# Transnormer attention and MLP mixer on one core: whole-tile attention for the first pair, reordered copies, earlier last stores

## The chip, the cores and the metric

The kernel runs on one core of a Trainium2 chip. The metric is the device time of one execution in microseconds (us). A core has a matrix engine (TensorE, PE in the profile, with its weight loads shown apart as PEld), a vector engine (DVE), a scalar engine (ACT), a general engine (POOL), and queues that issue DMAs (SP's, and ACT's own). Each engine runs its instructions in the order in which they were written; semaphores make one wait for another.

## The reference

For 8 batches of 576 tokens, with 8 heads of 64 columns:

```
kv  = einsum('bhsd,bhse->bhde', k, v)            # 64x64 per head
out = einsum('bhsd,bhde->bhse', q, kv)
x   = out / sqrt(mean(out*out, -1) + 1e-6) * g_norm   -> (8, 576, 512)

h   = relu(x^T @ w_tok1) @ w_tok2                # 576 -> 256 -> 576 tokens
u   = x + h^T
out = u + relu(u @ w_ch1) @ w_ch2                # 512 -> 1536 -> 512 channels
```

All activations are float32, and the MLP's weights come as float64 words, which the kernel decodes to float32 itself.

## The kernel before

**Pairs and tiles.** Batches are worked on in four pairs. Each batch has four tiles of 128 tokens and a rest of 64; the rests of a pair share a ninth tile. The work of a pair is: `kv` (k^T v per head, for one half of a batch's heads), `evict` (L348, from PSUM to `kvp`), `attend` (L357, q times kv), `gain` (L386, the product with g_norm, on DVE), `square` (L394, on ACT), `total` (L407, row sums on DVE), `mean`, `sqrt`, `invert` (L415 to L431), and then the scaling of x by the inverse root, on ACT as eight instructions of 64 columns (`scale`, L433) or on POOL as one (`scale_pool`, L440). Then `token_mixing` (L462): `tok1` into the four banks of the PSUM pool "h", a ReLU on ACT, and `tok2`, which either starts from zero (DVE then adds x) or is seeded: x is copied into PSUM first (`seed`, L483, on ACT), and the result is copied back by ACT.

**Quarters.** `attend` works by quarters of the array: 64 rows times 64 columns. `kvp` holds the 64x64 blocks of two heads above each other, and a step covers two tiles: one of its two banks (PSUM pool "o") gets the even heads of both tiles, the other the odd heads.

**The order.** The order on every engine is written out by hand, as lists of short names that `play` (L1018) runs from left to right: `start` (first pair's attention), `middle` (first pair's mixing with the second pair's attention), two `steady` lists and `last`. In the names, `kv00` is batch 0 of the pair, first half of the heads; `e00` its eviction; `l00` a load of k and v; `a0` to `a3` the attention of two tiles each, `a4` that of the rests; `g`, `q`, `t` gain, square and total; `m`, `r`, `i` mean, root and inverse of a group; `s` and `p` the scaling on ACT and on POOL; `h00` to `h11`, `hr` are `tok1`, `z2` is a seed and `u2` a `tok2`; `j14` is 14 small matmuls that only keep PE busy; `f` fetches a block of channel weights. A digit alone takes so many steps of the `rounding` stream, which decodes the channel weights block by block: an ACT scaling (L163) and six DVE instructions (L166 to L191); the scaling of the next block is issued with the fifth of them, the fetch of a later one with the last. The decoding of `w_tok2` is `w3x` and `w4x` in `middle`.

**After the mixing.** Channel mixing follows group by group as two nested fast matrix products of seven products each. `outer` (L722) builds one level; `put(place, ...)` sets a step beside a numbered product, `PLACE` orders the seven. With `onto=True`, for the very last of them (L883), its results are added straight to the output tile `xg` ("take", "write" and "put_on" are these additions). `store` (L985) and `store_rest` (L994) write the output: for the last group each issues one DMA on SP's queue and one on ACT's. Their places for the last group are in L967 to L970:

```
for place, steps in ((40, [xadd(1, 0, 4)]), (43, [xadd(0, 1, 6)]), (44, [radd(7, 6)]),
                     (46, [xadd(1, 0, 7)]), (47, [xadd(1, 1, 7)]), (49, [xadd(0, 1, 5)]),
                     (50, [xadd(1, 1, 5), do(store, g, xg, 1)]),
                     (52, [do(store_rest, xg, 1)]), (56, [do(store_rest, xg, 0)])):
```

Of the kernel before, what the change touches and what calls it, by code (L numbers as in the profile page):

```python
# [19 lines left out]
def kernel(  # L20
# [81 lines left out]
    v_in = [inp.tile([P, JJ, DH], F32, name=f"v_in{i}") for i in range(4)]  # L102
    kvp = [inp.tile([P, HP, D], F32, name=f"kvp{i}") for i in range(2)]
    u_dram = [dram.tile([J * P, DM], F32, name=f"u_dram{g}") for g in range(NG)]
# [226 lines left out]
    def attention(pair, groups):  # L331


        bank, stat, kv_ps = {}, {}, {}

        def kv(side, half):
            n = 4 * pair + 2 * side + half
            kk, vv = k_in[n % 4], v_in[n % 4]

            o = kv_ps[side, half] = ps["kv"].tile([P, 2, D], F32, name="ps_kv")  # L340
            for i in range(2):
                for j in range(JJ):
                    for h in range(2):
                        at = ds(i * P + h * D, D)
                        matmul(o[ds(h * D, D), i], lhsT=kk[:, j, at], rhs=vv[:, j, at],
                               start=(j == 0), stop=(j == JJ - 1), skip_group_check=True)

        def evict(side, half):  # L348
            o = kvp[side][:, 2 * half:2 * half + 2]
            if pair == 0:  # L350
                keep(nc.vector.tensor_copy(o, kv_ps[side, half]))
            else:
                copy(o, kv_ps[side, half])

        def attend(c):  # L357
            o = [ps["o"].tile([P, 2, HP, D], F32, name="ps_o", tag="o") for _ in range(2)]
            side = c // 2
            for t in range(2):  # L360
                for hp in range(HP):
                    for n in range(2):
                        for h in range(2):
                            r = ds(h * D, D)
                            matmul(o[h][ds(n * HF, HF), t, hp],
                                   lhsT=qT[2 * pair + side][r, hp, ds((2 * (c % 2) + t) * P + n * HF, HF)],
                                   rhs=kvp[side][r, hp], start=True, stop=True)
            for h in range(2):
                bank[c, h] = o[h].rearrange("p t k d -> p (t k) d")

        def attend_rem():
            o = [ps["o"].tile([P, HP, D], F32, name="ps_r", tag="o") for _ in range(2)]
            for hp in range(HP):
                for side in range(2):
                    for h in range(2):
                        r = ds(h * D, D)
                        matmul(o[h][ds(side * HF, HF), hp], lhsT=qT[2 * pair + side][r, hp, LO:],
                               rhs=kvp[side][r, hp], start=True, stop=True)
            for h in range(2):
                bank[4, h] = o[h]  # L380


        number = lambda c: HP if c == 4 else 2 * HP
        sq = {}

        def gain(c, h):  # L386
            if (pair, c) not in X:
                n = 1 if c == 4 else 2
                X[pair, c] = xps[pair % 2].tile([P, n, DM], F32, name="x", tag=f"x{n}",
                                                bufs=4 if n == 2 else 1)  # L390
            x = X[pair, c].rearrange("p t (k h d) -> p (t k) h d", h=2, d=D)[:, :, h]
            keep(nc.vector.tensor_mul(x, bank[c, h], g_sb.to_broadcast([P, number(c), D])))  # L392
# [8 lines left out]
        def stats_of(c):  # L401

            g = group(c)
            at = sum(2 * number(i) for i in g if i < c)
            return [t[:, ds(at, 2 * number(c))].rearrange("p (h k) o -> p h k o", h=2) for t in stat[g]]

        def total(c, h):  # L407
            g = group(c)
            if g not in stat:
                stat[g] = [stats.tile([P, sum(2 * number(i) for i in g), 1], F32, name=name)  # L410
                           for name in ("ms", "root", "inv")]
            keep(nc.vector.tensor_reduce(stats_of(c)[0][:, h], sq[c, h], axis=AX.X, op=ALU.add))  # L412
# [11 lines left out]
        def invert(g):  # L424
# [6 lines left out]
            keep(nc.vector.reciprocal(inv, root))  # L431

        def scale(c, t):  # L433
            x = X[pair, c][:, t].rearrange("p (k h d) -> p k h d", h=2, d=D)
            inv = stats_of(c)[2][:, :, ts(t, HP)]
            for k in range(HP):
                for h in range(2):
                    keep(nc.scalar.activation(x[:, k, h], x[:, k, h], AF.Copy, scale=inv[:, h, k]))  # L438

        def scale_pool(c, t):  # L440
            x = X[pair, c][:, t].rearrange("p (k h d) -> p k h d", h=2, d=D)
            inv = stats_of(c)[2][:, :, ts(t, HP)].rearrange("p h k o -> p k h o")
            keep(nc.gpsimd.tensor_mul(x, x, inv.to_broadcast([P, HP, 2, D])))  # L443

# [6 lines left out]
        for c in range(5):  # L451
            steps[f"a{c}"] = do(attend, c) if c < 4 else attend_rem
            for h in range(2):
# [7 lines left out]

    def token_mixing(pair, seeds):  # L462
        h1, acc = {}, {}
# [25 lines left out]
        def tok2(i):  # L489
            if i not in seeds:  # L490
                acc[i] = ps["h"].tile([P, DM], F32, name="ps_u", tag="h")
            first = i not in seeds
# [229 lines left out]
    def outer(place, size, mul, to, base=None, act=copy, onto=False):  # L722
# [56 lines left out]
        at(2, "c", False, True, lambda: take(0, 0, "c", act))  # L779
        put(place + PLACE[7] + 2, do(put_on, 1, 1, "u3"), do(write, 1, 1, "b", "u3"))  # L780
        at(4, "a", False, True, lambda: take(1, 0, "a", copy) if onto else read(to(1, 0), 1, 0))
# [79 lines left out]
    def channel2(g, n0):  # L861
# [104 lines left out]
        else:  # L966
            for place, steps in ((40, [xadd(1, 0, 4)]), (43, [xadd(0, 1, 6)]), (44, [radd(7, 6)]),  # L967
                                 (46, [xadd(1, 0, 7)]), (47, [xadd(1, 1, 7)]), (49, [xadd(0, 1, 5)]),
                                 (50, [xadd(1, 1, 5), do(store, g, xg, 1)]),
                                 (52, [do(store_rest, xg, 1)]), (56, [do(store_rest, xg, 0)])):  # L970
                put(b + place, *steps)
# [69 lines left out]
    for t in [t for pair in zip(k_in, v_in) for t in pair]:  # L1041
        keep(nc.gpsimd.memset(t[HF:, J], 0.0))

    root = stats.tile([P, 1], F32, name="root")
# [9 lines left out]
    for block in tok1[2:] + tok2:  # L1054
# [13 lines left out]
    middle = [  # L1068
# [6 lines left out]
    def steady(n0, n1):  # L1075
        return [
            "kv00 l00 e00 1 -s40", "h00 3", "kv01 l01 e01 1", "h01 3", f"a0 q00 g01 q01 g00 {n0}",
# [3 lines left out]
            "u6 t30 t31 m2 r2 1 i2 p20 p21 s30", f"u7 1 s31 {n1}", "u8 2"]  # L1081
# [3 lines left out]
    mixings = [token_mixing(p, (2, 4, 6) if p < B // 2 - 1 else range(2, 9)) for p in range(B // 2)]  # L1085
    more = {f"w{n}{k}": f for n, b in enumerate(tok1 + tok2) for k, f in enumerate(b)}
# [13 lines left out]
    for n in range(1, B // 2 - 1):  # L1100
        play(steady(*((2, 0), (2, 1))[n - 1]), attention=attentions[n + 1], mixing=mixings[n], before=attentions[n],
             rounding=rounding)
# [15 lines left out]
    def turn(i):  # L1118
# [6 lines left out]
    last = [  # L1125
        "h00 c0 2 -s40 2", "h01 c1 2", "h10 c2 2", "h11 c3 2", "hr 1", "u0 z2 1", "u1 z3 1", "u2 z4",
        "u3 z5 1", "u4 z6 1", "u5 z7 1", "u6 z8 1", "u7 c4", "u8"]
    more = {f"c{i}": do(turn, i) for i in range(J)}
# [95 lines left out]
```

## Time and profile before

| | |
|---|---|
| median of 3 runs | 813.64 us (813.44 to 814.81) |
| profiled execution, own time | 815.8 us |
| its span | 813.9 us |
| PE busy | 786.6 us (97%) |
| PE's weight loads busy | 689.5 us (85%) |
| DVE busy | 681.5 us (84%) |
| ACT busy | 308.1 us (38%) |
| POOL busy | 77.0 us (9%) |
| HBM | 214 GB/s over the span |

The span goes from the first to the last recorded instruction of one profiled execution; a little time lies around it. Stages, by PE's timeline: `start` to about 42.7 us, `middle` to 84.6, the two `steady` lists to 127.9 and 173.5, `last` to 206.5, and the channel mixing to the end. In a row of the profile, "x<-ps_o" names what is written and read, "x8" counts records, and the bracket gives the idle time before it on that engine with what ended it ("issue" where no wait is shown). One fp32 matmul leaves two records on PE.

### The profile page before, as it was taken

The numbers are of one execution on the slowest core, as the hardware profiler recorded it, in microseconds if no ns is written. First come the engines' busy times: TensorE is split into PE (matmuls) and PEld (weight loads), VectorE is DVE, ScalarE is ACT, GpSimd is POOL, SyncE is SP. The second block draws the span as 40 slices with busy tenths as digits, with TensorE's granted clock in tenths as the row PEclk, the third lists the DMA queues.
The fourth block names the chain that finished last, engine by engine and source line by source line (L and its number), as shares of the span: only waits on it lengthen the run. The fifth ranks groups of instructions, "written<-read, shape, count | busy, mean of one in ns | idle before, by whom it ended". The sixth has DMA issues, their size and how long they took to land.

```text
span 813.9 us, 18057 instructions
## 1 busy us (share of the span) xinstructions
PE 786.6 (97%) x7204; PEld 689.5 (85%) x7204; DVE 681.5 (84%) x1308; ACT 308.1 (38%) x863; POOL 77.0 (9%) x72
## 2 busy tenths in 40 slices
PE   5799999999999999999999999999999999999996
PEld 5445555443788899999999999999999999999996
DVE  3577999999786978987997997897898899799686
ACT  1466667583220034243234233333424323423431
POOL 1100101010000011003003003001100200300300
PEclk9999999999999999999999999999999999999998
DMA  9999999336458567468658638737836855764542
GB/s 286 293 337 294 358 360 347 130 129 178 151 200 274 198 203 242 144 207 233 198 172 255 212 123 279 236 118 230 283 125 213 259 166 196 235 195 147 195 142 82
DMA packets 97348, 175.54 MB, mean 216 GB/s; under 512 B 7024, under 2 KB 54128, under 8 KB 97264
## 3 DMA queue, kind: packets, MB, share of 16 engines
q1 hardware_dynamic: 95584, 172.65, 65.3%
q10 hardware_dynamic: 1680, 1.74, 0.7%
q8 instruction: 57, 0.93, 0.5%
q14 instruction: 27, 0.22, 0.1%
HBM read 137.79 MB, written 36.57 MB: 214 GB/s over the span
## 4 chain that ended last, share of the span: by engine, by line
PE 84%; DVE 8%; DMA 4%; ACT 3%; issue 1%; ACTq 0%; DVEq 0%
PE ps_a L127 37%; PE ps_b L127 18%; PE ps_c L127 9%; PE ps_v L127 4%; PE ps_w L127 4%; PE ps_h L127 4%; PE ps_u L127 4%; ACT x L438 2%; DMA qT<-in_q_dram 1%; DMA v_in<-in_v_dram 1%; PE ps_o L127 1%; DMA k_in<-in_k_dram 1%; DVE ms L412 1%; DVE x L392 1%; PE ps_kv L127 1%
## 5 line engine op out<-in xcount | busy, mean ns | idle before, releaser
L124 ACT COPY u<-ps_a 128x128 f32<-128x128 f32 (+1 forms) x160 | 56.2, 351 | 156.6 <-PE ps_a L127 156.6
L118 POOL TENSOR_TENSOR v<-v,v 128x384 f32<-128x384 f32 (+1 forms) x48 | 61.4, 1300 | 534.4 <-ACT v L124 494.6
L127 PE MATMUL ps_b<-uT,sums 128*128 128x128 f32 x672 | 86.2, 276 | 0.0
L127 PEld LDWEIGHTS ps_b<-uT,sums 128*128 128x128 f32 x672 | 80.7, 192 | 0.2
L118 DVE TENSOR_TENSOR v<-v,v 128x768 f32<-128x768 f32 (+1 forms) x86 | 79.4, 930 | 1.1
L127 PE MATMUL ps_a<-uT,w_ch 128*128 128x128 f32 x576 | 78.8, 275 | 0.0
L124 ACT COPY ps_c<-ps_a 128x128 f32<-128x128 f32 (+1 forms) x80 | 27.0, 337 | 129.5 <-PE ps_a L127 129.5
L127 PE MATMUL ps_u<-h,w_tok 128*128 128x512 f32 (+1 forms) x160 | 69.7, 620 | 3.8 <-DVE w_tok L118 1.9
L118 DVE TENSOR_TENSOR v<-ps_b,u 128x384 f32<-128x384 f32 x112 | 61.3, 547 | 12.7 <-PE ps_b L127 10.8
L127 PEld LDWEIGHTS ps_a<-uT,w_ch 128*128 128x128 f32 x576 | 71.5, 192 | 0.4
L127 PE MATMUL ps_h<-x,w_tok 128*128 128x512 f32 (+1 forms) x160 | 67.3, 612 | 1.5 <-POOL x L443 1.5
L118 DVE TENSOR_TENSOR uT<-uT 128x512 f32<-128x512 f32 (+4 forms) x103 | 63.0, 627 | 0.8
L127 PE MATMUL ps_a<-uT,w 128*128 128x128 f32 x432 | 60.0, 275 | 0.0
L438 ACT ACTIVATE x<-x,inv 128x64 f32<-128x64 f32 x208 | 52.2, 338 | 11.3 <-DVE inv L431 11.3
L127 PEld LDWEIGHTS ps_u<-h,w_tok 128*128 128x128 f32 (+1 forms) x160 | 25.1, 183 | 35.1 <-issue 27.2
L127 PEld LDWEIGHTS ps_a<-uT,w 128*128 128x128 f32 x432 | 54.0, 192 | 0.0
L127 PEld LDWEIGHTS ps_h<-x,w_tok 128*128 128x128 f32 (+1 forms) x160 | 26.0, 190 | 32.3 <-issue 27.2
L121 ACT ACTIVATE v<-v 128x384 f32<-128x384 f32 (+1 forms) x86 | 42.5, 529 | 22.9 <-DVE v L118 22.5
L118 DVE TENSOR_TENSOR xg<-xg,r 128x512 f32<-128x512 f32 x74 | 49.9, 684 | 0.6
L118 DVE TENSOR_TENSOR sv<-v 128x384 f32<-128x384 f32 x80 | 43.3, 550 | 8.0 <-ACT v L121 8.0
L127 PE MATMUL ps_a<-sums,sv 128*128 128x128 f32 x336 | 47.0, 276 | 0.0
L127 PE MATMUL ps_a<-uT,sums 128*128 128x128 f32 x336 | 46.8, 276 | 0.0
(133 smaller groups left out, 1560.2 us busy)
## 6 DMA issues: line engine op xcount, KB each, us to landing
sums<-sums SPq DMA_DIRECT2D x112, 576.0 KB, 4.0
qT<-in_q_dram SPq DMA_DIRECT2D x8, 1152.0 KB, 9.4
xt<-u_dram SPq DMA_DIRECT2D x36, 256.0 KB, 3.7
blocks<-y SPq DMA_DIRECT2D x72, 128.0 KB, 2.6
uT<-blocks SPq DMA_DIRECT2D x36, 256.0 KB, 4.7
xg<-u_dram SPq DMA_DIRECT2D x18, 512.0 KB, 4.8
k_in<-in_k_dram SPq DMA_DIRECT2D x16, 512.0 KB, 9.4
u_dram<-x SPq DMA_DIRECT2D x16, 512.0 KB, 4.9
```

Of the source, the lines that this page charges most:

```text
L118: keep(engine.tensor_tensor(out=o, in0=a, in1=b, op=op))
L121: keep(nc.scalar.activation(o, a, AF.Relu))
L124: keep(nc.scalar.copy(o, a))
L127: keep(nc.tensor.matmul(*a, **kw))
L392: keep(nc.vector.tensor_mul(x, bank[c, h], g_sb.to_broadcast([P, number(c), D])))
L412: keep(nc.vector.tensor_reduce(stats_of(c)[0][:, h], sq[c, h], axis=AX.X, op=ALU.add))
L438: keep(nc.scalar.activation(x[:, k, h], x[:, k, h], AF.Copy, scale=inv[:, h, k]))
```

## The change

- **First pair by whole tiles.** For pair 0, `kvp` holds a block-diagonal 128x128 block per two heads (its two off-diagonal blocks are zero: two PSUM tiles are cleared by DVE at the start and only their diagonal blocks written). A new `attend_tile` covers one tile with four 128x128 matmuls into one bank, in the natural order of heads. Gain, square and total work by tile. The other pairs keep the quarters, with `kvp`'s first 64 columns.
- **The order of `start`** is new: attention, gain and square tile by tile; most of the first batch's `tok1` stands together behind `kv11`, with more small matmuls (`j6`, `j2`); seven of nine scalings go to POOL instead of four.
- **`steady`**: `u6`'s copy stands in front of `s11` (and other names change lines: `s01`, `s10`, z6), and the number of rounding steps at two places becomes (3, 1) and (0, 0) instead of (2, 0) and (2, 1).
- **`last`**: the first two `tok2` use the banks of pool "o", and the seeds stand one step earlier.
- **The end**: the sum for rows 256 and up and their stores stand two places earlier, one addition one place later, and the step of the seventh product one place earlier in the last fast product.

```diff
-    kvp = [inp.tile([P, HP, D], F32, name=f"kvp{i}") for i in range(2)]
+    kvp = [inp.tile([P, HP, P], F32, name=f"kvp{i}") for i in range(2)]
...
+        whole = pair == 0
...
-            o = kv_ps[side, half] = ps["kv"].tile([P, 2, D], F32, name="ps_kv")
+            if whole:
+                o = kv_ps[side, half] = zeroed[half]
+            else:
+                o = kv_ps[side, half] = ps["kv"].tile([P, 2, P], F32, name="ps_kv", tag="kv")
...
-                        matmul(o[ds(h * D, D), i], lhsT=kk[:, j, at], rhs=vv[:, j, at],
+                        matmul(o[ds(h * D, D), i, ds(h * D if whole else 0, D)], lhsT=kk[:, j, at],
+                               rhs=vv[:, j, at],
...
+        def attend_tile(c, t):
+            side = c // 2
+            o = ps["o"].tile([P, DM], F32, name="ps_o", tag="o")
+            bank[c, t] = o.rearrange("p (h d) -> p h d", d=D)
+            for hp in range(HP):
+                matmul(o[:, ts(hp, P)], lhsT=qT[2 * pair + side][:, hp, ts(2 * (c % 2) + t, P)],
+                       rhs=kvp[side][:, hp], start=True, stop=True)
+
+        def attend_tile_rem():
+            o = ps["o"].tile([P, DM], F32, name="ps_r", tag="o")
+            bank[4, 0] = o.rearrange("p (h d) -> p h d", d=D)
+            for hp in range(HP):
+                for side in range(2):
+                    matmul(o[ds(side * HF, HF), ts(hp, P)],
+                           lhsT=qT[2 * pair + side][:, hp, LO:],
+                           rhs=kvp[side][:, hp], start=True, stop=True)
...
-    def token_mixing(pair, seeds):
+    def token_mixing(pair, seeds, aside=()):
...
             if i not in seeds:
-                acc[i] = ps["h"].tile([P, DM], F32, name="ps_u", tag="h")
+                n = "o" if i in aside else "h"
+                acc[i] = ps[n].tile([P, DM], F32, name="ps_u", tag=n)
...
-        put(place + PLACE[7] + 2, do(put_on, 1, 1, "u3"), do(write, 1, 1, "b", "u3"))
+        put(place + PLACE[7] + (1 if onto else 2), do(put_on, 1, 1, "u3"), do(write, 1, 1, "b", "u3"))
...
-                                 (46, [xadd(1, 0, 7)]), (47, [xadd(1, 1, 7)]), (49, [xadd(0, 1, 5)]),
-                                 (50, [xadd(1, 1, 5), do(store, g, xg, 1)]),
+                                 (46, [xadd(1, 0, 7)]), (47, [xadd(1, 1, 7)]), (48, [xadd(1, 1, 5), do(store, g, xg, 1)]),
+                                 (50, [xadd(0, 1, 5)]),
...
+    zeroed = [ps["kv"].tile([P, 2, P], F32, name="ps_kv", tag="kv") for _ in range(2)]
+    for t in zeroed:
+        keep(nc.vector.memset(t, 0.0))
...
-        "a0 q00 g01 q01 g00 t00 t01 m0 r0", "a1 g11 q10 i0 g10 q11 p00 s01 t10 t11 m1 r1",
-        "kv10 e10 i1 p10 s11", "h000 h001", "kv11 e11", "h002 h003",
-        "a2 q20 g21 q21 g20 t20 t21 m2 r2", "h010 h011", "a3 g31 q30 i2 g30 q31 p20 s21 t30 t31 m3 r3",
-        "h012", "a4 i3 p30 s31 q40 g41 q41 g40 t40 t41 m4 r4", "h013 w21 i4 s40 lq0 l10 l11"]
+        "a00 g00 q00", "a01 g01 q01 t00", "a10 g10 q10 t01 m0 r0", "a11 g11 q11 t10 i0 p00 p01",
+        "kv10 j6 t11 m1 r1 e10 i1 s10 p11", "kv11 j2 e11", "h000 h001 h002 h003", "a20 g20 q20", "a21 g21 q21 t20",
+        "h010 t21 m2 r2", "a30 g30 q30 i2 p20", "a31 g31 q31 t30", "h011 t31 m3 r3 p21", "a40 i3 p30 g40 q40 p31",
+        "h012 h013 t40 m4 r4 w21 i4 s40 lq0 l10 l11"]
...
-            "u0 i0 1", "kv11 l11 e11", "u1 1 s00", "u2 z4 1", "a2 q20 g21 q21 g20 s01", "u3 t20 t21",
-            "u4 1 z6", "a4 q40 g41 q41 g40 lq0 s10", "u5 t40 t41 1", "a3 q30 g31 q31 g30 lq1 s11",
-            "u6 t30 t31 m2 r2 1 i2 p20 p21 s30", f"u7 1 s31 {n1}", "u8 2"]
+            "u0 i0 1", "kv11 l11 e11", "u1 1 s00", "u2 z4 1", "a2 q20 g21 q21 g20", "u3 s01 t20 t21",
+            "u4 z6 1", "a4 q40 g41 q41 g40 lq0", "u5 s10 t40 t41 1", "a3 q30 g31 q31 g30 lq1",
+            "u6 s11 t30 t31 m2 r2 1 i2 p20 p21 s30", f"u7 1 s31 {n1}", "u8 2"]
...
+    mixings = [token_mixing(p, (2, 4, 6)) for p in range(B // 2 - 1)]
+    mixings.append(token_mixing(B // 2 - 1, range(2, 9), (0, 1)))
...
-        play(steady(*((2, 0), (2, 1))[n - 1]), attention=attentions[n + 1], mixing=mixings[n], before=attentions[n],
+        play(steady(*((3, 1), (0, 0))[n - 1]), attention=attentions[n + 1], mixing=mixings[n], before=attentions[n],
...
-        "h00 c0 2 -s40 2", "h01 c1 2", "h10 c2 2", "h11 c3 2", "hr 1", "u0 z2 1", "u1 z3 1", "u2 z4",
-        "u3 z5 1", "u4 z6 1", "u5 z7 1", "u6 z8 1", "u7 c4", "u8"]
+        "h00 c0 2 -s40 2", "h01 c1 2", "h10 c2 2", "h11 c3 2", "hr z2 1", "u0 z3 1", "u1 z4 1", "u2 z5",
+        "u3 z6 1", "u4 z7 1", "u5 z8 1", "u6 1", "u7 c4", "u8"]
```

More of the change, by code (lines that the diff above doesn't have):

```diff
@@ L344, in kv @@
                         at = ds(i * P + h * D, D)
-                        matmul(o[ds(h * D, D), i], lhsT=kk[:, j, at], rhs=vv[:, j, at],
+                        matmul(o[ds(h * D, D), i, ds(h * D if whole else 0, D)], lhsT=kk[:, j, at],
+                               rhs=vv[:, j, at],
                                start=(j == 0), stop=(j == JJ - 1), skip_group_check=True)
         def evict(side, half):
-            o = kvp[side][:, 2 * half:2 * half + 2]
-            if pair == 0:
-                keep(nc.vector.tensor_copy(o, kv_ps[side, half]))
-            else:
-                copy(o, kv_ps[side, half])
+            n = P if whole else D
+            o, i = kvp[side][:, 2 * half:2 * half + 2, :n], kv_ps[side, half][:, :, :n]
+            if whole:
+                keep(nc.vector.tensor_copy(o, i))
+            else:
+                copy(o, i)
+        def attend_tile(c, t):
[13 more added lines that the diff above has]
+                           rhs=kvp[side][:, hp], start=True, stop=True)
         def attend(c):
@@ L366, in attend @@
                                    lhsT=qT[2 * pair + side][r, hp, ds((2 * (c % 2) + t) * P + n * HF, HF)],
-                                   rhs=kvp[side][r, hp], start=True, stop=True)
+                                   rhs=kvp[side][r, hp, :D], start=True, stop=True)
             for h in range(2):
@@ L377, in attend_rem @@
                         matmul(o[h][ds(side * HF, HF), hp], lhsT=qT[2 * pair + side][r, hp, LO:],
-                               rhs=kvp[side][r, hp], start=True, stop=True)
+                               rhs=kvp[side][r, hp, :D], start=True, stop=True)
             for h in range(2):
                 bank[4, h] = o[h]
-        number = lambda c: HP if c == 4 else 2 * HP
+        number = lambda c: HP if c == 4 and not whole else H
+        parts = lambda c: 1 if c == 4 and whole else 2
         sq = {}
@@ L390, in gain @@
                                                 bufs=4 if n == 2 else 1)
-            x = X[pair, c].rearrange("p t (k h d) -> p (t k) h d", h=2, d=D)[:, :, h]
+            if whole:
+                x = X[pair, c][:, h].rearrange("p (h d) -> p h d", d=D)
+            else:
+                x = X[pair, c].rearrange("p t (k h d) -> p (t k) h d", h=2, d=D)[:, :, h]
             keep(nc.vector.tensor_mul(x, bank[c, h], g_sb.to_broadcast([P, number(c), D])))
@@ L403, in stats_of @@
             g = group(c)
-            at = sum(2 * number(i) for i in g if i < c)
-            return [t[:, ds(at, 2 * number(c))].rearrange("p (h k) o -> p h k o", h=2) for t in stat[g]]
+            n = lambda i: parts(i) * number(i)
+            at = sum(n(i) for i in g if i < c)
+            return [t[:, ds(at, n(c))].rearrange("p (h k) o -> p h k o", h=parts(c)) for t in stat[g]]
         def total(c, h):
@@ L409, in total @@
             if g not in stat:
-                stat[g] = [stats.tile([P, sum(2 * number(i) for i in g), 1], F32, name=name)
+                stat[g] = [stats.tile([P, sum(parts(i) * number(i) for i in g), 1], F32, name=name)
                            for name in ("ms", "root", "inv")]
@@ L431, in invert, with inv_of @@
             keep(nc.vector.reciprocal(inv, root))
+        def inv_of(c, t):
+            inv = stats_of(c)[2]
+            if whole:
+                return inv[:, t].rearrange("p (k h) o -> p k h o", h=2)
+            return inv[:, :, ts(t, HP)].rearrange("p h k o -> p k h o")
         def scale(c, t):
             x = X[pair, c][:, t].rearrange("p (k h d) -> p k h d", h=2, d=D)
-            inv = stats_of(c)[2][:, :, ts(t, HP)]
+            inv = inv_of(c, t)
             for k in range(HP):
                 for h in range(2):
-                    keep(nc.scalar.activation(x[:, k, h], x[:, k, h], AF.Copy, scale=inv[:, h, k]))
+                    keep(nc.scalar.activation(x[:, k, h], x[:, k, h], AF.Copy, scale=inv[:, k, h]))
         def scale_pool(c, t):
             x = X[pair, c][:, t].rearrange("p (k h d) -> p k h d", h=2, d=D)
-            inv = stats_of(c)[2][:, :, ts(t, HP)].rearrange("p h k o -> p k h o")
-            keep(nc.gpsimd.tensor_mul(x, x, inv.to_broadcast([P, HP, 2, D])))
+            keep(nc.gpsimd.tensor_mul(x, x, inv_of(c, t).to_broadcast([P, HP, 2, D])))
         steps = {}
@@ L451, in attention @@
         for c in range(5):
-            steps[f"a{c}"] = do(attend, c) if c < 4 else attend_rem
-            for h in range(2):
+            if whole:
+                steps |= {f"a{c}{t}": do(attend_tile, c, t) if c < 4 else attend_tile_rem
+                          for t in range(parts(c))}
+            else:
+                steps[f"a{c}"] = do(attend, c) if c < 4 else attend_rem
+            for h in range(parts(c)):
                 steps |= {f"{n}{c}{h}": do(f, c, h) for n, f in zip("gqt", (gain, square, total))}
@@ L1078, in steady @@
             "h10 1 t00 t01 2", "h11 4", "hr 2 z2", "a1 q10 g11 q11 g10 1", "kv10 l10 e10 t10 t11 m0 r0 1",
[2 rows of a table removed]
-            "u6 t30 t31 m2 r2 1 i2 p20 p21 s30", f"u7 1 s31 {n1}", "u8 2"]
[2 rows of a table added]
+            "u6 s11 t30 t31 m2 r2 1 i2 p20 p21 s30", f"u7 1 s31 {n1}", "u8 2"]
     attentions = [attention(0, ((0,), (1,), (2,), (3,), (4,)))]
     attentions += [attention(p, ((0, 1), (2, 3, 4))) for p in range(1, B // 2)]
-    mixings = [token_mixing(p, (2, 4, 6) if p < B // 2 - 1 else range(2, 9)) for p in range(B // 2)]
+    mixings = [token_mixing(p, (2, 4, 6)) for p in range(B // 2 - 1)]
+    mixings.append(token_mixing(B // 2 - 1, range(2, 9), (0, 1)))
     more = {f"w{n}{k}": f for n, b in enumerate(tok1 + tok2) for k, f in enumerate(b)}
```

## The prediction

> **What bounds the kernel now.** I read the slices first.
>
> ```profile
> PE   5799999999999999999999999999999999999996
> PEclk9999999999999999999999999999999999999998
> DMA  9999999336458567468658638737836855764542
> ```
>
> A slice is 20.3 us. TensorE (PE) is full from the third slice on: from 206.5 us (the channel mixing) its passes follow each other without a gap, so no edit can gain there except behind its last matmul. What is left is the first 206 us, where PE has holes and the DMA engines are full for seven slices. Next the chain of waits over the first 60 us.
>
> ```profile
> 19.64 11.20 DMA qT<-in_q_dram
> ...
> 35.25 2.86 issue
> ...
> 48.12 2.03 ACT x L438 x8
> ...
> 57.76 0.77 DVE w_tok L118
> 58.53 0.14 issue
> 58.66 2.02 PE ps_u L127 x2
> ```
>
> Batch 1's q lands at 30.84 us and starts `a2`. From there the chain runs through normalising pair 0 to the scaling of tile 8 (48.12), behind which ACT and DVE decode `w_tok2`; its end (58.53) releases the second half of `u0`. On it lies a hole of 2.86 us in `a3` that no wait explains. The holes on PE and what ended them:
>
> ```profile
> 58.66 4.51 PE L127 MATMUL ps_u<-h,w_tok 128*128 128x512 f32 x6 [1.92 <-DVE w_tok L118]
> ...
> 160.88 1.98 PE L127 MATMUL ps_u<-h,w_tok 128*128 128x512 f32 x4 [0.74 <-ACT ps_u L124]
> ...
> 166.91 1.16 PE L127 MATMUL ps_o<-kvp,qT 64*64 64x64 f32 x64 [1.12 <-ACT sq L396]
> ...
> 197.58 9.00 PE L127 MATMUL ps_u<-h,w_tok 128*128 128x512 f32 x24 [1.10 <-ACT ps_u L124]
> ```
>
> Beside these: 1.32 before 79.85 (in `middle`, whose list is unchanged) and 0.26 before 121.39. And what a hole does to the clock (a stretch and its length, busy time of PE, its loads, DVE, ACT and POOL, then granted clock, DMA share and GB/s):
>
> ```profile
> 35.30:38.20 2.90, 0.09 (x2) 0.09 (x1) 0.00 (x0) 0.60 (x2) 0.00 (x0) 1.00 1.11 273
> 38.20:42.70 4.50, 4.50 (x38) 2.04 (x37) 3.73 (x11) 2.75 (x10) 1.06 (x1) 0.62 1.11 297
> 58.60:63.20 4.60, 4.54 (x10) 1.78 (x14) 2.90 (x5) 1.90 (x3) 0.00 (x0) 0.63 1.09 345
> ```
>
> After the holes the clock was 0.62 and 0.63 of full.
>
> **Part 1, whole tiles for pair 0.** A quartered step took 1.16 us for two tiles (64 rows of 64x64). A whole tile is 4 matmuls, 8 passes of 128x128 (each matmul leaves two records). No such attention row exists; the nearest is the channel mixing's "PE ps_a L127 x12" at 1.34 us in the chain, 0.112 us a pass with its weight load hidden: 0.9 us a tile, not 0.58. The bound above is 0.275 us a pass (mean duration of one such row, no overlap), 2.2 us a tile; I take 0.9. Here a rule speaks against the change: the Trainium skill, TensorEngine Tiling (Array Packing), Overview, gives four independent 64x64 tiles, up to 2x for each small dimension. By it alone pair 0 pays 9 tile-times x 0.32 = 2.9 us. By the chain PE isn't what ends last: what counts is when DVE and ACT get a tile.
>
> Now the sums, with L392 0.63, L396 0.60, L412 0.60, the four short DVE steps of `i` 0.95, POOL's scaling 1.06, ACT's eight scalings 2.02, a `tok1` matmul 0.95. Clearing two PSUM tiles at the start lies before the first matmul at 6.92; the eviction grows from 128 to 256 columns, about +0.14 (L166's 0.43 for 512 against L351's 0.29), under the 0.89 that DVE idles at 10.5, and `j10` keeps PE until 18.34 anyhow. Before batch 1's q: `a00` starts at 18.34, a bank turns round in 0.9 + 0.63 + 0.60, `a11` ends near 22.5, `kv10` at 23.9; `kv11` waits for v, landed at 26.58 (landings are from the trace's landing events), ends at 28.0. The four `h00` now stand together behind it: 28.4 to 32.2. So `a20` starts at 32.2, later than the 30.97 of before. Then `a20`, `a21`, `h010`, `a30`, `a31`, `h011`, `a40` end at 38.6; on DVE `t21` ends at 35.9, `i2` 37.7, `t31` 39.6, `i3` 41.0, `g40` 41.6, `i4` 44.2 (before 48.1). Scaling tile 8 ends at 46.3, decoding is a fixed 8.4 us behind it (before 50.14 to 58.53): 54.7. PE: `kv00` of `middle` from 40.5 (its k and v landed at 39.78), `h10`, `kv01`, `h11`, `hr` to 52.3, `a0` to 53.4, `u0` half to 54.3. The hole is 0.4 us, not 1.92: **3.9 us**.
>
> The clock: rule and row differ. The skill, TensorE: Matmul & The Clock Gate, Part 1, puts the drop after an idle window of 3.4 us; here 1.92 us of hole did it (while 1.47 us before 20.96 did not). The six passes at 58.66 took 4.52 us where six at full clock take 2.7 (ps_h x8 in 3.63). By the rule a short hole costs nothing and the gain stays 3.9; by the row 1.3 us more goes with the hole (DVE idled 1.71 at 63.21, waiting for PE). I take the row: **5.2 us** at the end of `u1`, carried through `middle`.
>
> The 2.86 us: a 16 KB packet of the instruction queue ran at 35.35, when PE had executed 961 records, matmuls and loads, and stopped. I take it as late instructions. Pair 0 drops 200 of PE's 64x64 passes and as many loads, so record 961 comes at 53 instead of 35 and the crowd of short instructions before it is gone: taken as zero, other end 2.9.
>
> **What takes part of it back.** DMA is full from 6 to 74.4 us (block f3 lands at 74.44) with no hole to close; only the dip at 75 to 79 can go, some 1.8 to 3.4 us. So phase two of the loads comes about 3.4 us sooner, not 5.2. Which load is tight? q, k and v of this phase have 5 us and more at every use. Block 5 of the channel weights doesn't:
>
> ```profile
> 103.78 0.60 ACT L121 ACTIVATE h<-ps_h 128x512 f32<-128x512 f32 x1 [5.86 <-PE ps_h L127]
> 104.64 1.58 ACT L121 ACTIVATE h<-ps_h 128x512 f32<-128x512 f32 x3 [0.26 <-PE ps_h L127]
> 106.09 0.96 ACT L163 ACTIVATE w_ch<-raw 128x768 f32<-128x768 f32 x1
> ```
>
> It was issued at 96.07 and landed at 104.5. The new `steady(3, 1)` moves one rounding step forward, and with it this L163 **in front of** the four L121 in ACT's queue. Queued behind it: the ReLUs, seed z2, the squares of `a1`; `u0` waits for the ReLUs. Due at 98.6 (103.78 - 5.2), block 5 lands at 101.1: ACT holds the ReLUs to 102.0, `u0` waits 1.3 us, and the squares' delay of 2.4 us comes back at `a3`, about 0.9. So **2.0 us** are given back; of 5.2, 3.2 stay, about what DMA allows. Ends: 0 (block in time) and 3.
>
> **Part 2, copies and squares before scalings.** In the first steady stage 0.26 can go; the step added before `i0` uses 0.69 us that DVE idled at 107.4. I count 0, as the hold above overlays it. In the second, two steps fewer stand at `a0`, but the same number was done earlier: DVE is busy without a hole to 152.24, so only the absorbed 0.55 comes off `i0`, z4 and the squares: **0.5** of 1.86. Putting u6's copy ahead of `s11` swaps 0.5 with 2.0 us on ACT, both before the same root: nothing.
>
> **Part 3, last mixing.** u0 and u1 take the attention banks, idle by then; z4 no longer needs DVE's add at 196.17, the hole of 1.10 before 197.58 goes. One step more on DVE here is balanced by one less at the stage before: **1.1**. The next thing late is `uT`'s sums, done at 204.9 and needed at 207.2.
>
> **Part 4, the end.**
>
> ```profile
> 807.45 2.47 SPq L115 DMA_DIRECT2D out_dram<-xg  x4
> 807.45 2.75 ACTq L115 DMA_DIRECT2D out_dram<-xg  x4
> ...
> 807.92 0.29 DVE L118 TENSOR_TENSOR xg<-ps_b,xg 128x128 f32<-128x128 f32 x1
> ```
>
> Four stores stand on each queue, 0.62 us on SP and 0.69 on ACT, all issued from 807.45: the last leaves at 810.2, 2 us after its data (808.2). Now two of them issue at 805.7, after L943's add moved in front, one at 807.6, the last at 808.4 to 809.1. DVE's ten operations keep their sum and end at 808.0. **1.1**; the last flight stays.
>
> **Sum**: 3.2 + 0.5 + 1.1 + 1.1 = 5.9 us. The profiled execution took 815.8 with a span of 813.9; runs have a median of 813.64, so I take the difference off that: **807.7**.
>
> **Rivals.** (a) Block 5 lands in time: nothing given back, 0.26 more: 805.4. For it: 1.6 us of slack before, and ACT idle 5.86 there; against it: full DMA. (b) PE's instructions come late again elsewhere (`a0` of `middle`): 2.9 off the start, but what DMA caps anyway is lost first: net about 2, 809.7. (c) A whole tile isn't pipelined and takes 2.2 us: nine tiles x 1.3 = 11.7, less 1.3 that `kv11` waits anyhow, less 3.9, gives 6.5 lost at the start; with 2.7 from the other parts +3.8: **817.4**, slower. It decides from about 1.8 us a tile; against it stands 0.112 a pass in every channel row. (d) The start's gain doesn't outlast the loads at all, `middle` being held by them: 0 instead of 3.2 and the other 2.7 stay: 810.9. For it: DMA full to 74; against: its k and v landed at 39.78 and 43.97, uses now 40.5 and 45.4, its q at 49.4 for 52.3, all in time though by little.
>
> **Chances.** Forecast 0.46, (a) 0.21, (b) 0.18, (c) 0.08, (d) 0.07. The range 804.6 to 811.0 takes (a), (b) and the forecast with its ends. 0.2% is 1.6 us, about what a measurement can tell from no change: faster 0.88 (the first three and 0.03 of (d)), same 0.04 (the rest of (d)), slower 0.08 (c).
>
> **To look for.** `ps_o` x8 in 0.9 us in the start; no hole of 2.9 near 35; `i4` near 44; u0's second half near 54.7 and no clock of 0.5 there; a hole of some 1.3 before u0 near 102 with L163 ahead of L121 (none: rival a); no hole near 192; stores at 805.7. It would be wrong if `a20` came after 34, or if a new hole over 1.9 us halved the clock.

## The result, and the profile after

| | before | after |
|---|---|---|
| median of the runs beside each other | 814.11 us (813.44 to 814.81, n=4) | 808.0 us (807.63 to 808.49, n=4) |
| ratio to before | | 0.9925 [0.9908, 0.9942] |
| profiled execution, its span | 815.8, 813.9 us | 807.63, 805.8 us |
| mean granted clock of that execution | 0.993 | 0.999 |

A second series gave 807.47 (806.29 to 808.15, n=6), ratio 0.9915 [0.9901, 0.9929]; the median of all ten is 807.6. Predicted: 807.7. The two profiled executions lie further apart (8.2 us) than the medians (6.1): that of before stood about 2 us above its own median.

The slices of the profile after:

```profile
PE   6999999999999999999999999999999999999997
...
PEclk9999999999999999999999999999999999999999
...
DMA  9999998436458567468467648738836855863642
```

The 7 in PE's second slice is a 9, and the DMA engines are full for six slices instead of seven. The chain of waits through the start (start, length, what):

```profile
26.13 1.39 PE ps_kv L127 x40
...
44.22 2.02 ACT x L475 x8
...
53.85 0.77 DVE w_tok L118
54.75 2.81 PE ps_u L127 x6
```

Tile 8 is scaled at 44.22 (before 48.12), `w_tok2` is decoded at 54.6 (58.5), and no "issue" of 2.86 us is left. PE's timeline, the rows that answer to those of before:

```profile
54.75 2.81 PE L127 MATMUL ps_u<-h,w_tok 128*128 128x512 f32 x6 [0.55 <-DVE w_tok L118]
...
101.97 1.98 PE L127 MATMUL ps_u<-h,w_tok 128*128 128x512 f32 x4 [0.57 <-ACT h L121]
...
155.89 1.98 PE L127 MATMUL ps_u<-h,w_tok 128*128 128x512 f32 x4 [0.26 <-ACT ps_u L124]
...
161.93 1.16 PE L127 MATMUL ps_o<-kvp,qT 64*64 64x64 f32 x64 [1.12 <-ACT sq L425]
...
184.37 15.87 PE L127 MATMUL ps_u<-h,w_tok 128*128 128x512 f32 x40
```

The six passes take 2.81 us instead of 4.51, the hole in front of them is 0.55 instead of 1.92. At 101.97 there is a new hole. That at 155.89 was 0.74, that at 161.93 is as long as before, and the products of the last mixing run unbroken. The clock, in two stretches (length, PE, its loads, DVE, ACT, POOL, clock, DMA share, GB/s):

```profile
38.20:42.70 4.50, 4.50 (x51) 2.60 (x48) 3.15 (x9) 1.21 (x3) 3.07 (x4) 1.00 1.06 356
54.60:57.50 2.90, 2.75 (x7) 1.06 (x7) 2.90 (x6) 1.91 (x3) 0.00 (x0) 1.00 1.04 390
```

Where it was 0.62 and 0.63, it is 1.00. Block 5 of the channel weights on ACT, and the end (SP, ACT, DVE):

```profile
100.00 0.94 ACT L163 ACTIVATE w_ch<-raw 128x768 f32<-128x768 f32 x1 [7.70 <-DMA raw<-in_moe_w_ch_dram]
100.84 2.05 ACT L121 ACTIVATE h<-ps_h 128x512 f32<-128x512 f32 x4
...
799.58 2.96 SPq L115 DMA_DIRECT2D out_dram<-xg  x4
799.58 3.23 ACTq L115 DMA_DIRECT2D out_dram<-xg  x4
...
801.70 0.29 DVE L118 TENSOR_TENSOR xg<-ps_b,xg 128x128 f32<-128x128 f32 x1
```

L163 now holds the four ReLUs, which is the new hole. The last store leaves at 802.8, 1.1 us behind DVE's start of its last sum (801.70); before it was 2.3 behind (810.2 against 807.92).

The traces side by side, as moves of the same instruction on PE: first `kv` 0.24 us sooner, `a1` of `middle` 5.61, start of the second steady stage 4.50, start of the last mixing 4.98, start of the channel mixing 6.35, last product 6.61, end of the span 8.1. The lead of 5.61 falls to 4.50 over the first steady stage, so 1.1 us is given back there; the rest adds to it.

### The profile page after: what moved, and what is told of

It is laid out like the page before. It is cut to its first block, busy times and chain, and to the rows that moved or that the text cites. A ratio compares the mean times of both kernels' runs of the same rounds, so it can differ in the third digit from the quotient of the medians.

```text
span 805.8 us, 17651 instructions
## 1 busy us (share of the span) xinstructions
PE 788.6 (98%) x7012; PEld 694.4 (86%) x7012; DVE 683.3 (85%) x1308; ACT 302.2 (38%) x838; POOL 79.6 (10%) x75
## 4 chain that ended last, share of the span: by engine, by line
PE 83%; DVE 6%; DMA 5%; ACT 3%; SPq 1%; issue 1%; ACTq 0%; DVEq 0%
PE ps_a L127 37%; PE ps_b L127 19%; PE ps_c L127 9%; PE ps_v L127 5%; PE ps_w L127 4%; PE ps_u L127 4%; DMA v_in<-in_v_dram 3%; PE ps_h L127 2%; ACT x L475 1%; SPq L115 1%; DMA raw<-in_moe_w_ch_dram 1%; DMA k_in<-in_k_dram 1%; DVE ms L442 1%; DVE part L187 1%; DVE x L421 1%; PE ps_o L127 1%
## 5 line engine op out<-in xcount | busy, mean ns | idle before, releaser
L127 PE MATMUL ps_u<-h,w_tok 128*128 128x512 f32 (+1 forms) x160 | 68.0, 608 | 1.6 <-ACT h L121 0.6
L475 ACT ACTIVATE x<-x,inv 128x64 f32<-128x64 f32 x184 | 46.0, 336 | 9.6 <-DVE inv L461 9.6
```

Source lines behind the costliest of these rows:

```text
L127: keep(nc.tensor.matmul(*a, **kw))
```

## Experiments

The theory is that of the prediction: four parts whose gains add. Its rivals were that the start's gain is swallowed by the loads, or that it belongs to the order alone, or to the tiles alone. All kernels below were timed against before, whose medians in the four series were 813.5 to 813.8. "After" is the changed kernel.

| kernel | median us (range, n) | ratio to before |
|---|---|---|
| part 1 undone | 810.9 (809.24 to 813.34, 11) | 0.997 [0.9961, 0.9979] |
| part 2 undone | 807.43 (807.09 to 807.61, 5) | 0.9927 [0.9914, 0.9941] |
| part 3 undone | 808.38 (807.51 to 809.33, 5) | 0.9939 [0.9926, 0.9951] |
| parts 2 and 3 undone | 808.95 (808.21 to 810.2, 5) | 0.9945 [0.9933, 0.9956] |
| part 4 undone | 809.3 (808.47 to 810.36, 5) | 0.9951 [0.9939, 0.9964] |
| whole tiles, order of before | 811.9 (810.55 to 813.21, 11) | 0.9977 [0.9966, 0.9988] |
| quarters, new order | 812.43 (809.67 to 813.55, 12) | 0.9979 [0.9969, 0.999] |
| whole tiles, order of before, tile 7 on POOL | 808.17 (808.13 to 809.07, 5) | 0.9936 [0.9924, 0.9949] |
| quarters, order of before, tile 7 on POOL | 810.57 (808.47 to 812.16, 6) | 0.9959 [0.9942, 0.9975] |
| after, numbers (2, 2), (0, 0) | 807.3 (807.03 to 808.08, 5) | 0.9918 [0.9905, 0.9932] |
| after, three edits in its lists | 806.17 (804.82 to 806.65, 4) | 0.9904 [0.9889, 0.9919] |

### The parts, each undone

**Part 1.** Pair 0 by quarters, `start` as before, all else as after:

```diff
-        "a00 g00 q00", "a01 g01 q01 t00", "a10 g10 q10 t01 m0 r0", "a11 g11 q11 t10 i0 p00 p01",
...
+        "a0 q00 g01 q01 g00 t00 t01 m0 r0", "a1 g11 q10 i0 g10 q11 p00 s01 t10 t11 m1 r1",
...
```

> The changed kernel with its first part undone: pair 0 again by quarters and in the order of before, all else as changed. The prediction's theory (start and middle 5.2 us sooner on TensorE, 2.0 of it given back at block 5 of the channel weights, 3.2 kept): 811.2 us against 808.0 with it. Corrected by the two traces (5.6 sooner at the end of middle, 1.1 given back): 812.5. Rival, the start's gain is swallowed by the loads: 808.0 to 808.5. A second rival, that the hole of 2.86 us near 35 us was of that one execution and not of the program: no such hole in this trace, and then 809.5 to 811.

810.9, which is 3.3 us above the 807.6 of after: the prediction's 811.2 holds, the 812.5 "corrected" by traces does not. The trace has the stop of 2.86 us at the same place as before (62 of `a3`'s 64 records), the hole of 1.89 before `u0`'s second half, and two stretches of half clock. So the stop belongs to the program. But this traced run took 813.34 and was the slowest of eleven. In it `a1` of `middle` starts at 63.55, 6.06 later than in after, and the span ends 5.7 later: of the start's gain only 0.3 is lost on the way.

**Part 2** and **part 3**, and both (part 2 with the names in the `steady` lists moved back too):

```diff
-        play(steady(*((3, 1), (0, 0))[n - 1]), ...
+        play(steady(*((2, 0), (2, 1))[n - 1]), ...
...
-    mixings.append(token_mixing(B // 2 - 1, range(2, 9), (0, 1)))
...
-        "hr z2 1", "u0 z3 1", "u1 z4 1", "u2 z5",
+        "hr 1", "u0 z2 1", "u1 z3 1", "u2 z4",
```

> The changed kernel with its second part undone: steady lists and their numbers as before, the scaling of block 5 again behind the ReLUs. Theory: the first steady stage no longer waits for that scaling, u0 has no hole of 0.57 near 102 and a3 comes about 1.1 us sooner, but the second stage has its 1.86 us of holes again instead of 1.38 (0.5 lost): 807.4. Rival, the give-back is due to the loads in whatever order the queue stands: 808.5. The whole span of both is 807.0 to 809.0.

> The changed kernel with its third part undone: u0 and u1 of the last mixing again in the banks of pool h, the seeds one step later. Theory: the hole of 1.1 us before the last mixing's products of u2 and u3 is back, 809.1 (the traces' difference over this stage is 1.37: 809.4). Rival, the hole is hidden by what follows at 207 us (the sums of uT): 808.0.

> The changed kernel with its second and third parts both undone (first and fourth stay). The third alone left a hole of 0.19 us before u2 of the last mixing, not 1.10. Theory: the steady numbers of the change take one decoding step (0.69) away from in front of the addition that the seed waits for, so either part alone closes most of this hole; with both undone it is 1.0 to 1.1 again, and the time is 1.0 to 1.1 above the version with the second part alone undone (807.4): 808.4 to 808.6. Rival, the hole of before came with its slower start: below 0.3 here, 807.5.

With part 2 undone block 5's scaling starts at 99.95 behind the ReLUs, the hole before `u0` is gone, that at `u4` of the second stage is 0.74 again, and the time is 807.43 as expected. So block 5's hold costs about what the second stage gains. Part 3 undone moved the time by 0.8, not 1.1, and not all of that is part 3: in the traces the last mixing itself is only 0.45 longer (32.10 us against 31.65), while the traced run with part 3 undone, which is its median, waits 0.76 us at 500.67 for `sums` to land, and after does not. The hole tells why it is so little (PE and DVE, last mixing, first part 3 undone, then parts 2 and 3):

```profile
189.60 0.68 DVE L118 TENSOR_TENSOR x<-ps_u,x 128x512 f32<-128x512 f32 x1
190.20 0.68 DVE L166 TENSOR_SCALAR w_ch<-w_ch 128x1024 f32<-128x1024 f32 x1
...
191.01 9.00 PE L127 MATMUL ps_u<-h,w_tok 128*128 128x512 f32 x24 [0.19 <-ACT ps_u L124]
```

```profile
189.57 0.69 DVE L166 TENSOR_SCALAR w_ch<-w_ch 128x1024 f32<-128x1024 f32 x1
190.17 0.68 DVE L118 TENSOR_TENSOR x<-ps_u,x 128x512 f32<-128x512 f32 x1
...
191.58 9.00 PE L127 MATMUL ps_u<-h,w_tok 128*128 128x512 f32 x24 [1.10 <-ACT ps_u L124]
```

The numbers (3, 1) and (0, 0) hold four decoding steps where (2, 0) and (2, 1) hold five. One step (L166, 0.69 us) therefore no longer stands on DVE in front of the addition that frees a bank for the seed. It closes 0.9 of the 1.10; either part closes nearly the whole hole, and only with both undone it is back, as expected. The time, 808.95, lies above the 808.4 to 808.6 expected. Both parts together are worth 1.35 (808.95 less 807.6).

**Part 4.**

```diff
-        (48, [xadd(1, 1, 5), do(store, g, xg, 1)]), (50, [xadd(0, 1, 5)]),
+        (49, [xadd(0, 1, 5)]), (50, [xadd(1, 1, 5), do(store, g, xg, 1)]),
...
-        put(place + PLACE[7] + (1 if onto else 2), ...
+        put(place + PLACE[7] + 2, ...
```

> The changed kernel with its fourth part undone: the last additions and stores at their places of before. Theory: four stores on each queue from the same moment, the last one 1.1 us later than now: 809.1. By the traces (0.24 us of idle TensorE, then 7.4 less 6.6 at the last store): also 809.0. Rival, that the last stores' flight and not their issue sets the end: 808.0 to 808.3.

809.3: 1.7 us above after, more than either forecast's 1.0 to 1.1. The stores on ACT's queue in this run:

```profile
801.68 2.75 ACTq L115 DMA_DIRECT2D out_dram<-xg  x4
```

The span holds 7.0 us from PE's last product (801.11) to its end (808.1), against 5.6 in after (800.27 to 805.8). PE's 0.24 is the hole before that product. Of the other 1.4, the last store leaves 0.8 sooner behind the product in after, and what follows it is 0.6 shorter: 3.66 us here and 3.73 in before, 2.99 to 3.21 in the twelve traces with the stores moved.

The parts so measured are 3.3, 1.35 and 1.7; their sum, 6.35, is near the 6.1 between the medians, so they add within the spread.

### The start: tiles, order, and one move

The order of before with whole tiles, and the new order with quarters (all other parts as after):

```diff
+        "a00 a01 q00 g01 q01 g00 t00 t01 m0 r0", "a10 a11 g11 q10 i0 g10 q11 p00 s01 t10 t11 m1 r1",
...
+        "h012", "a40 i3 p30 s31 q40 g40 t40 m4 r4", "h013 w21 i4 s40 lq0 l10 l11"]
```

```diff
+        "a0 g00 q00 g01 q01 t00", "a1 g10 q10 t01 m0 r0 g11 q11 t10 i0 p00 p01",
...
+        "a3 g30 q30 i2 p20 g31 q31 t30", "h011 t31 m3 r3 p21", "a4 i3 p30 g40 q40 g41 q41 p31",
```

> The changed kernel with pair 0 by whole tiles but in the order of before (the two tiles of a step side by side, the first batch's first products spread out, five tiles scaled on ACT instead of two). Theory of the prediction: the stop of 2.86 us of TensorE goes with the crowd of short instructions, so tiles alone remove it (no hole without a cause near 35 us), i4 ends near 45.3 instead of 44.2, and of the start's 2.9 us in the medians about 2 stay: 808.9. Rival, the order does the work and the tiles cost what packing saved (2.9 us by the rule): 811 to 812.

> The changed kernel with pair 0 by quarters but in the new order (two tiles of a step, gain and square by bank in the order of the change, scalings mostly on POOL). Theory: 487 weight loads after the start TensorE stops again for 2.9 us, now 48 records into a3, half the clock follows, and the time is 810.0 to 811.0. Rival, the order does the work whatever the tile: no stop that matters, i4 near 44.5, 808.0 to 808.5.

Neither alone brings anything: 811.9 and 812.43, no better than the 810.9 with neither. The first expectation was wrong, and the timeline shows what it missed (ACT's two rows, then PE's; whole tiles in the order of before):

```profile
41.44 2.02 ACT L475 ACTIVATE x<-x,inv 128x64 f32<-128x64 f32 x8 [1.10 <-DVE inv L461]
43.36 0.57 ACT L425 ACTIVATE sq<-ps_r 128x512 f32<-128x512 f32 x1
...
57.20 4.34 PE L127 MATMUL ps_u<-h,w_tok 128*128 128x512 f32 x6 [2.64 <-DVE w_tok L118]
```

PE no longer stops, and `a40` is done at 39.1. But in the list of before `s31` stands in front of `q40`: ACT scales tile 7 for 2 us first, the ninth tile's square waits, `i4` ends at 46.6, decoding at 57.1, and PE waits 2.64 us. The clock is 0.63 after that.

With quarters in the new order (PE, then a stretch of the windows):

```profile
36.11 0.92 PE L127 MATMUL ps_o<-kvp,qT 64*64 64x64 f32 x46 [0.27 <-ACT sq L396]
38.00 0.46 PE L127 MATMUL ps_o<-kvp,qT 64*64 64x64 f32 x16 [0.97 <-issue]
```

```profile
38.70:45.50 6.80, 6.03 (x38) 2.40 (x36) 5.86 (x18) 2.12 (x5) 3.94 (x4) 0.50 0.72 219
```

PE stops after 48 records of `a3` (2 + 46), the very place expected. The 487 of the expectation are 475 weight loads and 12 other instructions of PE's own queue (11 semaphore waits and a drain); with 474 matmuls they make 961 records, and here it is 961 again (474 loads, 13 others, 474 matmuls). The stop is 0.97 us instead of 2.86, yet the clock is halved for 6.8 us, `a1` of `middle` starts at 62.40 (61.47 with tiles alone, 57.49 in after), and the time lies above the 810.0 to 811.0 expected. Of its twelve runs, the only one with a mean clock of 1.00 was the fastest (809.67); all others had 0.993 to 0.997.

So one move should do for the tiles what the whole new order does:

```diff
-        "h012", "a40 i3 p30 s31 q40 g40 t40 m4 r4", "h013 w21 i4 s40 lq0 l10 l11"]
+        "h012", "a40 i3 p30 p31 q40 g40 t40 m4 r4", "h013 w21 i4 s40 lq0 l10 l11"]
```

> Whole tiles in the order of before, with one instruction group moved: the second tile of the last pair of tiles (x of tile 7) is scaled on POOL as in the change, not on ACT in front of the ninth tile's square. Theory: in the version with it on ACT that scaling ran from 41.44 to 43.36 us, the square behind it and with it i4 (46.6) and the decoding of w_tok2 (57.06) came 2.0 to 2.5 us late; without it i4 ends near 44.3, the hole of 2.64 us before u0's second half shrinks below 0.8, no half clock follows it, and the time is 808.0 to 809.0. Rival, the whole new order is needed (the rest of the chain is as long): hole above 1.5 us, half clock, 810.5 to 812.

> The fourth corner: pair 0 by quarters in the order of before, but x of tile 7 scaled on POOL instead of ACT (all other parts as changed). Theory, tiles and this one move are both needed because each takes away another thing that sets i4: with quarters TensorE still stops for 2.86 us with two records of a3 to go, a4 comes after it whatever ACT does, i4 ends near 48.0, the half clock after the stop stays: 810.0 to 811.0, as with ACT (810.9). Rival, the move alone is worth its 3.7 us whatever the tile: 807.2 to 808.0.

With tiles it does: 808.17, 3.7 us less by one letter (3.3 by the ratios, as the two kernels stand in different series). The hole before `u0`'s second half is 1.17, where less than 0.8 was expected, and no half clock follows (PE):

```profile
55.48 2.81 PE L127 MATMUL ps_u<-h,w_tok 128*128 128x512 f32 x6 [1.17 <-DVE w_tok L118]
```

With quarters the same letter is worth 0.3 in the medians (810.57 for 810.9, within their spread):

```profile
38.02 0.27 PE L127 MATMUL ps_o<-kvp,qT 64*64 64x64 f32 x2 [2.86 <-issue]
...
57.38 3.70 PE L127 MATMUL ps_u<-h,w_tok 128*128 128x512 f32 x8
```

The stop of 2.86 us is where it was, half clock follows for 6.8 us, PE itself is the last to come (no hole before `u0`, `a1` at 61.01), and `i4`, at 46.5, isn't on the path. Its end was expected at 48.0; ACT's scaling had cost it 1.6 there too (48.1 in before), only hidden. The two traced runs differ by 2.95 us (813.34 and 810.39), for that of part 1 undone stood 2.4 above its median; the 0.3 can't be read off them.

The rest of the new order is worth about 0.6 (808.17 to 807.6), which these runs hardly separate.

### After again, and faster versions

> The changed kernel itself, on the chip and beside the kernels of this call, as their measure: 808.0 again, within 0.6.

807.47. Its trace has 1.32 us of hole before `u0` in the first steady stage, where the first one had 0.57: block 5 landed at 100.5 instead of 99.98. Two more kernels have the same `start`, `middle` and `steady`: with part 4 undone the hole was 1.35 (block 5 at 100.72), with part 3 undone there was none (99.32).

Two versions move decoding steps only. The first changes the numbers; the second also moves two steps of `middle` behind the ninth tile's gains:

```diff
-        play(steady(*((3, 1), (0, 0))[n - 1]), ...
+        play(steady(*((2, 2), (0, 0))[n - 1]), ...
```

```diff
-        "u5 t20 t21 2", "a4 q40 g41 q41 g40 lq0 l10 l11", "u6 t40 t41 2",
+        "u5 t20 t21", "a4 q40 g41 q41 g40 lq0 l10 l11 2", "u6 t40 t41 2",
...
-        play(steady(*((3, 1), (0, 0))[n - 1]), ...
+        play(steady(*((2, 1), (0, 0))[n - 1]), ...
...
-        "u3 z6 1", "u4 z7 1", "u5 z8 1", "u6 1", "u7 c4", "u8"]
+        "u3 z6 1", "u4 z7 1", "u5 z8 1", "u6 2", "u7 c4", "u8"]
```

> The changed kernel with the numbers of its steady lists at (2, 2) and (0, 0) instead of (3, 1) and (0, 0): the scaling of block 5 stands behind the ReLUs again, while the second stage keeps one step fewer at its start. Theory: the hole of 0.57 us before u0 and that of 0.21 before u4 go, about 1.1 us in the first steady stage, and nothing comes back: 806.9. Rival, the step moved behind u7 is late for the next stage: 807.5 to 808.0.

> The changed kernel with three edits in its lists: numbers (2, 1) and (0, 0) in the steady lists, the two decoding steps of middle behind the ninth tile's gains instead of in front of them, one more step at u6 of the last mixing. Theory: middle's hole of 1.33 us before a3 shrinks to some 0.3 (1.0 gained), the hold of block 5 goes (1.1), and one DVE step fewer ahead of u4 of the second stage keeps its hole near 0.5 to 0.8 instead of 1.24: 806.0 to 806.5 against 807.5 of the changed kernel. Rival, VectorE is the bound over both steady stages and what is gained before comes back there, or sums of the channel mixing land late: 807.0 to 807.8.

The first closes both holes of the first steady stage, but `u4` of the second then waits 1.24 us instead of 0.26, and 0.5 is lost at 698 us, where `sums` land late for their product: 807.3, between the two expectations, with the losses that the rival named. DVE bounds the second stage, and what PE gains before it comes back there, unless DVE is relieved too. The second does that (PE):

```profile
72.98 1.16 PE L127 MATMUL ps_o<-kvp,qT 64*64 64x64 f32 x64
...
154.61 1.99 PE L127 MATMUL ps_u<-h,w_tok 128*128 128x512 f32 x4 [0.51 <-ACT ps_u L124]
```

Middle's hole of 1.33 is gone, that of `u4` is 0.51, that before `u0` is gone, and one of 0.74 at `a3` (115.36) is new. 806.17 is 1.4 us below after and below before by 1.0%; its interval against before overlaps that of after, which wasn't timed beside it.

## Why the prediction was right, and where its terms were off

- **Whole tile 0.9 us**: right, 1.80 for two tiles in the chain (31.77), where quarters take 1.09 (57.56, `a1` of `middle`). So giving up the quarters does cost PE 0.36 us a tile (0.32 forecast), but nothing at the end, as argued: PE still waits 0.55 us for the decoding of `w_tok2`.
- **The way to 54.7**: `a20` 31.61 (predicted 32.2), `a40` ends 38.26 (38.6), `i4` 44.19 (44.2), decoded 54.61 (54.7), hole 0.55 (0.4), `a1` 5.61 sooner (5.2 at the end of `u1`). Right, with the half clock: the six passes took 2.81.
- **What makes it so was told too roughly.** The sum counted the new order and the tiles as one path. The four corners of tiles and order (810.9, 811.9, 812.43, 807.6), and sharper those of tiles and one letter (810.9, 811.9, 810.57, 808.17), show two limits lying over each other. Quarters bring the stop and half clock; `s31` in front of `q40` makes DVE's decoding late. Each hides the other's removal. The prediction saw the stop but not `s31`'s place.
- **The stop taken as zero**: right. The Trainium skill, Runtime: NRT & Kernel Launch, Instruction fetch mechanics, has instructions refilled in 16 KiB blocks, the crossing "mostly hidden". Here it was not: 2.86 us in three traces, at the same record each time, with a 16 KB instruction packet under way among full DMA engines. In all four kernels with quarters PE went on 1.47 to 1.51 us after the end of that packet (in before 38.11 and 36.64). In the ten traces with whole tiles the packet had ended by 46.7 us and record 961 ran without a stop at 52.1 to 53.0 us, as forecast (53). That the late packet is the cause fits all traces, but no run took it alone away. (PE dropped 192 matmul records, 7204 to 7012, not 200: the ninth tile takes eight matmuls.)
- **Given back 2.0: the upper end, by a path that was partly wrong.** The first steady stage took 43.25 us in before (84.63 to 127.88); in the four traces with after's `start`, `middle` and `steady` it took 44.37 and 45.11 (after), 43.80 (part 3 undone) and 45.15 (part 4 undone): 0.6 to 1.9 given back. The size depends on when block 5 lands. The prediction held phase one of the loads to be rigid ("DMA is full from 6 to 74.4 us ... with no hole to close") and so let block 5 land only 3.4 us sooner. But block f3 landed at 71.20 instead of 74.44: the share stayed above 1, but the same stretch carried 356 GB/s instead of 297, so a share of 1 is not the full rate. And block 5's issue moved with the computation by the whole 5.22 us (90.85 for 96.07); only its flight grew, from 8.45 us to 8.7 to 9.8. So it came at 99.3 to 100.7 instead of 101.1, and `u0` waited between nothing and 1.35 (1.3 predicted). From `a1` of `middle` to the end of the span, after took 748.3 and 749.1, part 1 undone 748.0: counted so, 0.3 to 1.1 is given back.
- **The median.** The sum was made on one execution and taken off the median. The executions differ by 8.2, the medians by 6.1; the traced one with part 1 undone, too, was 2.4 above its median. So a usual run of these two kernels loses about 2 us less than the traced one; where and how, no trace shows, and the mean clocks of the eleven runs (0.992 to 0.997, the traced one 0.995) don't tell them apart. This and the give-back, too large at the end of the span, cancel: part 1 measures 3.3 in medians, the forecast's 3.2. That the total came out within 0.3 us is in part luck.
- **Part 2, 0.5 in the second stage**: 0.48. **Part 3, 1.1 by the banks**: the hole went, but 0.9 of it by the step that part 2's numbers take away. "One step more on DVE here is balanced by one less at the stage before" was the wrong sentence: at the addition it is one less. Together 1.6 was forecast for the two, the hold of block 5 counted apart; 1.35 was measured, with the hold in it.
- **Part 4, 1.1**: 1.7. "The last flight stays" was wrong by 0.4 to 0.7, and PE's 0.24 had been left out.
- **Rivals**: none of (b) to (d) came; (a) is partly true: block 5 was late by less, and in one of the four traces not at all.

## What to carry to other kernels

When two things end at nearly the same time, taking one away shows nothing: only the 2x2 of both (here tiles and one scaling's queue) tells what each is worth. In an engine's queue, look at what stands in front of the instruction that a long chain waits for; moving one scaling to an idle engine was worth 3.7 us with whole tiles (and 0.3 while quarters held PE up). And where one profiled execution stands well above the median, find out which part of its time is its own before taking a difference off the median.

## What was not expected of the hardware

- PE stopped for 2.86 us with 961 records behind it (474 matmuls, 475 weight loads, 12 others) in before, with part 1 undone and with tile 7 on POOL, and for 0.97 us after 961 in the new order with quarters; in all four it went on about 1.5 us after a 16 KB instruction packet had ended.
- The clock: holes of 1.89, 1.92, 2.64 and 2.86 us were each followed by 3.41 us (or 6.83) of half clock; those of up to 1.48 that stood alone were not. Several short ones together were in one kernel (quarters in the new order: 1.43 and 0.27 at 21 us; 0.43, 0.27 and 0.97 at 35 to 38 us), while 1.47 and 0.25 at 21 us in before were not. In all fourteen traces the clock changes only at whole multiples of 3413 ns from its first change (stretches of full clock of 13653, 17067, 27307 and 47787 ns are 4, 5, 8 and 14 of them). Up to 205 us, the windows of this grid that a drop followed had PE idle for 0.50 to 0.84 of them, with one exception of 0.42 (from 35.31, quarters in the new order); the idlest window without a drop had 0.43. So about half a window idle is enough here, whether in one hole or several, and where a hole falls in the grid matters; PE's ends are modelled, and no sharper limit comes out. The Trainium skill, TensorE: Matmul & The Clock Gate, Part 1, gives a free-running window of 3413 ns, which the lengths of the half clock bear out (3413 and 6827 ns); that it takes an idle window of 3.4 us they don't.
- From the end of the last store's issue to the end of the span it was 3.7 us with four stores on each queue issued one behind the other, and 3.0 to 3.2 with the first two issued before.
